# Spectral filter, soft mixture of experts and gated feed-forward on one core: batch sums of the last chain moved to VectorE, weight loads moved to SyncE

## The chip, the cores and the metric

The kernel runs on one core of a Trainium2 chip. The metric is the device time of one execution in microseconds (us), the median over several runs. TensorE does the matrix products, VectorE and ScalarE read its results out of PSUM, GpSimd helps with elementwise work, and SyncE only issues DMA transfers; ScalarE and GpSimd can issue transfers too, each from its own queue, in program order with their other instructions.

## The reference

Cut to what matters (shapes: x 8 x 3072 x 256, w1 8 x 256 x 1024, w2 8 x 1024 x 256, gate and value weights 256 x 1536, output weights 1536 x 256):

```
Y = irfft(rfft(x, axis=1) * (filt_r + 1j * filt_i))      # per batch, along the sequence
x = Y.reshape(8 * 3072, 256)
logits = x @ phi                                          # 32 slots
d = exp(logits - logits.max(0)); d /= d.sum(0) + 1e-9     # over all 24576 tokens
slot_input = (d.T @ x).reshape(8, 4, 256)                 # 8 experts, 4 slots each
slot_out[e] = relu(slot_input[e] @ w1[e]) @ w2[e]
c = exp(logits - logits.max(1)); c /= c.sum(1) + 1e-9
x = c @ slot_out
out = (silu(x @ w_gate) * (x @ w_val)) @ w_out
```

## The kernel before, in words

The program is one list of instructions for each engine, in the order in which the Python code emits them. Nothing is reordered at run time: an engine works through its list and waits where a tile is not ready.

**Phase 1** (`phase1`, to 350 us) is the spectral part. 16 steps (batch and half of the columns) have 6 units each, so `units` has 96 entries `i`. `s2_unit` multiplies and filters, `tr_unit` and `phi_pair` transpose and form logits in the spectral domain two units later, `s1_chunk` prepares the next step. Beside the units a generator `chain(b, last)` runs for each batch: it is cut by `yield` into pieces, and `pump(1)` emits the next piece. The pieces are, in order: six transposes (tile `lh`, L354), a product with `inv` (L364, `us`), six transposes (`t4`), the logits (L391, then the maximum `cm` at L398 and the copies `lg`), the batch maximum `mb` (L411), subtraction and exponential (`dd`), a product back (L447, transposed into `bd`), a product with `fwd` (L459, `dt`), six transposes (L474, `dh`), and the slot product of 48 matrix instructions in six parts `k` with the batch's filtered rows `yt` (L482, copied to `sl`). Batches 0 to 5 store `sl` to DRAM; batch 6 and batch 7 are the two chains g6 and g7 at the end. In the last ten units `pump(1)` is called twice a unit, until g6 has done nine pieces. Behind the loop the two generators are advanced in an order written out by hand, `for g in (g6, g7, g6, g7, g7, g6, g7, g6, g6)`, and then g7 to its end.

The generator `combine()` joins the eight batches: weights exp(mb - max) for each batch, their normalisation, then the scaled sum of the eight `sl`. Before, the sum is made on TensorE: 28 matrix instructions with 32 columns (L548) for batches 0 to 6, and four (L502) that add batch 7. Its result `sp` goes into a block layout `stm`.

The expert weights w1 are 16 halves of 512 KB. 13 of them are issued by ScalarE in units 84, 90 and 91 into buffers that phase 1 has freed there, and 3 by SyncE behind the loop (all at L134). The eight w2 (1024 KB each, L770) are issued by SyncE in the order 6, 7, 0, then the gate weights `wg`, then 5, 4, 1, 2, 3 and the value weights `wv` (1536 KB each, L127). Each waits until the tiles of phase 1 at its address are read for the last time.

**Transition** (`transition`, 378 to 405 us): `stage1` (L812) multiplies the slots by w1, `turn` (L829) transposes, `stage2` (L837) multiplies by w2. Then the slot outputs are multiplied by the gate and value weights (L872, L883) into tiles `g4` and `v4`: rows of a rounded part and of its remainder. For the first 512 columns the remainder is formed on VectorE at L877, for the other 1024 columns 16 transfers (L895) copy the rows into place, 8 issued by SyncE and 8 by GpSimd.

**Phase 2** (`phase2`) has 576 items of 512 tokens x 128 hidden columns. Each: two matrix products G and V (L988, L989), SiLU (L991), product h (L997), split into `hi` and `lo` (L1004, L1005), and six output products (L1026) three or four items later. The output weights come in as 12 tiles; `load_out(f)` rounds one on ScalarE (L977) and forms its remainder on GpSimd (L978), one tile an item in items 0 to 11. The last 12 items end in another layout (`close`): four accumulators, each read by a ScalarE copy (L1060) and a VectorE sum (L1061), then four transfers on SyncE (L1069).

Of the kernel before, what the change touches and what calls it, by code (L numbers as in the profile page):

```python
# [20 lines left out]
NF = FF // 128  # L21
LAG = 4
EXP_AT = 17
HOLD = 9
# [55 lines left out]
def spectral_softmoe_glu_kernel(  # L80
# [56 lines left out]
    def phase1():  # L137
        with ExitStack() as c1:
# [4 lines left out]
            cvp = c1.enter_context(tc.tile_pool(name="cvp", bufs=1))  # L143
# [5 lines left out]
            ps_s1 = c1.enter_context(tc.tile_pool(name="ps_s1", bufs=1, space=PSUM))  # L149
            ps_x = c1.enter_context(tc.tile_pool(name="ps_x", bufs=2, space=PSUM))  # L150
            ps_t = c1.enter_context(tc.tile_pool(name="ps_t", bufs=1, space=PSUM))
            ps_l = c1.enter_context(tc.tile_pool(name="ps_l", bufs=1, space=PSUM))
            ps_c = c1.enter_context(tc.tile_pool(name="ps_c", bufs=1, space=PSUM))
# [154 lines left out]
            def chain(b, last):  # L308
# [15 lines left out]

                def pair(name):
                    if b == NB - 2 and name in ("dt", "dh"):
                        t = ytp.tile([128, 768], F32, tag="yt", name=name)
                        return [t[:, 0:512], t[:, 512:768]]
# [58 lines left out]
                cm = chp.tile([128, E], F32, tag="cm", name="cm")  # L387
# [9 lines left out]
                both = bass.AP(pl[0].tensor, pl[0].offset, [list(pl[0].ap[0]), [16, E], [512, 2], [1, 16]])  # L397
# [10 lines left out]
                if not last:  # L408
                    yield
                ps = small()  # L410
                pe.transpose(out=ps[0:32, 0:128], in_=cm, identity=ident)  # L411
                dve.tensor_reduce(
                    out=mb[:, b:b + 1],
                    in_=ps[0:32, 0:128].rearrange("p (g n) -> p g n", g=2)[:, :, 0:48],
# [22 lines left out]
                if last:  # L437
# [3 lines left out]
                bd = chp.tile([128, E, 32], F32, tag="lg", name="bd")  # L441
                pl = (ps_s1.tile([128, 1024], F32, tag="s1", name="cl") if last else small()).rearrange(
                    "p (g e n) -> p g e n", g=2, n=16
                )
                for h in range(2):
                    for g in range(2):
# [5 lines left out]
                        )  # L452
                for es in es2:
# [3 lines left out]
                for jj in range(NJ):  # L457
# [6 lines left out]
                    )  # L464
                dt_ = evac("dt", ps)
# [7 lines left out]
                for k in range(6):  # L473
                    pe.transpose(out=col(ps, k), in_=col(dt_, k), identity=ident)  # L474
                if last:
                    rb, pss = next(com)
                dh = evac("dh", ps)
                yield
                ps = two(True)[0] if b == NB - 2 else small()
                for k in range(6):  # L480
# [9 lines left out]
                    if k in (2, 5) and b == NB - 2:  # L490
# [5 lines left out]
                act.copy(sl, ps[:, 0:256])  # L496
                if b < NB - 2:
                    nc.scalar.dma_start(out=sld[:, b, :], in_=sl)
                if last:
                    next(com)  # L500
                    for d_ in range(2):
                        pe.matmul(  # L502
                            out=pss[d_][:, 0:32], lhsT=sl[:, d_ * 128:(d_ + 1) * 128], rhs=rb[:, b, :],
                            start=False, stop=True,
                        )
                        (dve.tensor_copy if d_ else act.copy)(sp[:, d_, :], pss[d_][:, 0:32])
# [10 lines left out]
            def combine():  # L517
# [5 lines left out]
                beta4 = chp.tile([128, NB, 1], F32, tag="beta4", name="beta4")  # L523
                dve.tensor_reduce(out=mx, in_=mb, axis=AX.X, op=ALU.max)
                dve.tensor_scalar(al, mb, mx, None, ALU.subtract)
                act.activation(al, al, AF.Exp)
                yield
# [4 lines left out]
                dve.tensor_scalar(al, al, sm, 2.0 / SEQ, ALU.mult, ALU.mult)  # L532
                yield
                rb = chp.tile([128, NB, 32], F32, tag="t4", name="rb")
                psb = ps_t.tile([128, 512], F32, tag="T", name="psb")
                pe.matmul(out=psb[:, 0:NB], lhsT=rep4[0:32, :], rhs=al)
                dve.tensor_copy(beta4[:, :, 0], psb[:, 0:NB])
                dve.tensor_tensor(
                    out=rb,
                    in0=rep4[:, None, 0:32].to_broadcast([128, NB, 32]),  # L540
                    in1=beta4.to_broadcast([128, NB, 32]),
                    op=ALU.mult,
                )
                pss = [ps_x.tile([128, 512], F32, tag="X", name="pss") for _ in range(2)]
                yield rb, pss
                for d_ in range(2):
                    for b in range(NB - 1):
                        pe.matmul(  # L548
                            out=pss[d_][:, 0:32],
                            lhsT=slots[b // 4][:, b % 4, d_ * 128:(d_ + 1) * 128],  # L550
                            rhs=rb[:, b, :],
                            start=(b == 0),
                            stop=False,
                        )
                yield

# [93 lines left out]
            xp += [cr.enter_context(tc.tile_pool(name=f"xp{k}", bufs=1, side="right")) for k in (1, 0)][::-1]  # L650
            load_x(0, 0)
# [52 lines left out]
            for i, (s, u) in enumerate(units):  # L704
# [18 lines left out]
                if (s, u) in ((2 * NB - 2, 0), (2 * NB - 1, 0)):  # L723
                    wt = xp[s % 2].tile([128, 2, 2, FE], F32, tag="x", name="w")
                    for k in range(2):
                        load_w1(nc.scalar, 2 * (s % 2) + k, enumerate(wt[:, k, t] for t in range(2)))
                if (s, u) == (2 * NB - 1, 0):
                    load_w1(nc.scalar, 4, [(t, sgp.tile([128, FE], F32, tag="sg", name="w")) for t in range(2)])
                if (s, u) == (2 * NB - 1, 1):
                    wt = bp[0].tile([128, 3, FE], F32, tag="b", name="w")  # L730
                    load_w1(nc.scalar, 5, ((0, wt[:, 0]), (1, wt[:, 1])))
                    load_w1(nc.scalar, 7, ((0, wt[:, 2]),))
                if i >= len(units) - 10:
# [9 lines left out]
            load_w1(nc.sync, 6, ((0, wt[:, 0]), (1, wt[:, 1])))  # L743
            load_w1(nc.sync, 7, ((1, wt[:, 2]),))
# [4 lines left out]
            for u in (4, 5):  # L749
                tr_unit(2 * NB - 1, u, dve.tensor_copy)  # L750
                next(g7)
            for g in (g6, g7, g6, g7, g7, g6, g7, g6, g6):
                next(g, None)
            for _ in g7:
                pass
# [5 lines left out]
    def transition():  # L761
# [13 lines left out]
        w2s[0] = one([128, 8, D], "w2_0")  # L775

# [9 lines left out]
        one([128, 10 * D], "pad")  # L786
# [8 lines left out]
        for e in (6, 7, 0):  # L795
            load_w2(e)
        flat_load(wg, wd[0], 128)
        for e in (5, 4, 1, 2, 3):
            load_w2(e)
        flat_load(wv, wd[1], 128)  # L800

# [67 lines left out]
        for w, dst in gates:  # L869
# [6 lines left out]
            for r in (32, 96):  # L876
# [262 lines left out]
```

## Time and profile before

| | |
|---|---|
| median of 3 runs | 1464.82 us (1464.5 to 1465.57) |
| the profiled execution | 1466.01 us |
| its span, first to last instruction | 1464.2 us, so 1.81 us lie around it |
| mean granted TensorE clock | 0.992 of full speed |

The span is what the trace explains; all times of the trace are counted from its start. A full clock is 2.4 GHz, and a granted clock of 0.50 is the lower level, 1.2 GHz.

### The profile page before, as it was taken

To read this page: it belongs to the slowest core of one execution; us is meant where nothing else is said; L and a number is where in the kernel's file an instruction comes from. 1 tells how busy PE (TensorE), PEld (TensorE's weight loads), DVE (VectorE), ACT (ScalarE), POOL (GpSimd) and SP (SyncE) were. 2 spreads that over 40 slices of the span, in tenths; PEclk is the share of its full clock that TensorE was granted. 3 is DMA by queue.
4 is the path that set the end of the run, shared out by engine and by line. 5 is a ranking of instruction groups with operands and counts; after the bars stand their busy time and mean duration, and the time that the engine had idled before them with its cause. 6 is when DMAs were issued, how large, how long until landed. Compare 5 with 4: busy or idle time off the path is not lost.

```text
span 1464.2 us, 22633 instructions
## 1 busy us (share of the span) xinstructions
PE 1414.5 (97%) x8446; PEld 1101.4 (75%) x8446; DVE 1147.1 (78%) x1776; ACT 905.0 (62%) x1650; POOL 243.4 (17%) x315
## 2 busy tenths in 40 slices
PE   4899999998999999999999999999999999999998
PEld 2566666665567888888888888888888888888887
DVE  2788888877188878878887897888779878877775
ACT  2466667764266667666766666676666667666664
POOL 0466666663030000000000000000000000000000
PEclk9999999999999999999999999999999999999999
DMA  9979888978721231231131112212210320221111
GB/s 230 158 121 165 148 135 145 185 156 338 281 50 19 37 67 24 37 61 30 30 59 40 29 31 56 40 29 44 55 29 15 73 40 16 54 47 21 24 29 30
DMA packets 178077, 116.26 MB, mean 79 GB/s; under 512 B 105136, under 2 KB 161328, under 8 KB 177840
## 3 DMA queue, kind: packets, MB, share of 16 engines
q1 hardware_dynamic: 170720, 102.37, 35.6%
q10 hardware_dynamic: 6800, 11.54, 2.7%
q8 instruction: 67, 1.10, 0.3%
q0 software_dynamic: 448, 0.92, 0.2%
q14 instruction: 42, 0.34, 0.1%
HBM read 68.13 MB, written 34.60 MB: 70 GB/s over the span
## 4 chain that ended last, share of the span: by engine, by line
PE 91%; DVE 4%; ACT 2%; DMA 1%; issue 1%; POOL 1%; SPq 0%; ACTq 0%; POOLq 0%; DVEq 0%
PE o L1026 52%; PE V L989 9%; PE G L988 9%; PE X L258 5%; PE s L230 4%; PE T L283 2%; PE L L291 1%; PE c L482 1%; DMA x<-in_x_dram 1%; DVE sg L238 1%; PE o L1048 1%; PE c L364 1%; DVE P L262 1%; PE h L812 1%; PE c L447 1%
## 5 line engine op out<-in xcount | busy, mean ns | idle before, releaser
L1026 PE MATMUL o<-hi,wo 128*128 128x512 f32 x2256 | 696.3, 390 | 2.7 <-POOL wo L978 2.7
L991 ACT ACTIVATE s<-G 128x512 f32<-128x512 f32 x576 | 344.7, 598 | 331.7 <-PE G L988 327.6
L997 DVE TENSOR_TENSOR h<-V,s 128x512 f32<-128x512 f32 x576 | 393.5, 683 | 154.6 <-ACT s L991 151.8
L1026 PEld LDWEIGHTS o<-hi,wo 128*128 128x128 f32 x2256 | 424.5, 188 | 91.3 <-POOL wo L978 3.0
L1026 PE MATMUL o<-lo,wo 128*128 128x512 f32 x1128 | 439.5, 390 | 0.0
L1005 DVE TENSOR_TENSOR lo<-h,hi 128x512 fp32r<-128x512 f32 x576 | 421.5, 732 | 1.1
L1004 ACT CAST hi<-h 128x512 fp32r<-128x512 f32 x576 | 354.2, 615 | 36.4 <-DVE h L997 35.1
L1026 PEld LDWEIGHTS o<-lo,wo 128*128 128x128 f32 x1128 | 212.0, 188 | 43.9
L989 PE MATMUL V<-c,v 128*128 128x512 f32 x576 | 224.9, 390 | 1.2 <-DVE h L997 1.2
L988 PE MATMUL G<-c,g 128*128 128x512 f32 x576 | 224.7, 390 | 0.3 <-ACT s L991 0.3
L258 PEld LDWEIGHTS X<-fwd,b 128*128 128x128 f32 x768 | 95.2, 195 | 57.0 <-issue 40.3
L989 PEld LDWEIGHTS V<-c,v 128*128 128x128 f32 x576 | 108.4, 188 | 25.0 <-DVE h L997 2.7
L988 PEld LDWEIGHTS G<-c,g 128*128 128x128 f32 x576 | 108.2, 188 | 24.4 <-ACT s L991 1.1
L238 DVE STREAM_TRANSPOSE sg<-s 128x1024 f32<-128x1024 f32 x64 | 78.9, 1236 | 58.4 <-PE s L230 56.7
L258 PE MATMUL X<-fwd,b 128*128 128x128 f32 x768 | 111.6, 289 | 2.2 <-ACT b L247 1.2
L935 POOL TENSOR_TENSOR lg<-lg,mx 96x1024 f32<-96x1024 f32 x7 | 16.8, 2405 | 550.3 <-DVE mx L933 550.3
L230 PE MATMUL s<-x,csm 48*64 48x512 f32 x512 | 73.7, 632 | 18.6 <-DMA x<-in_x_dram 16.6
L247 ACT COPY b<-sg 128x768 f32<-128x768 f32 x64 | 59.0, 925 | 52.8 <-DVE sg L238 52.6
L271 POOL TENSOR_TENSOR yt<-P 128x256 f32<-128x256 f32 x96 | 70.4, 734 | 117.7 <-DVE P L262 117.2
L1031 DVE STREAM_TRANSPOSE ot<-o 128x512 f32<-128x512 f32 x94 | 65.1, 714 | 29.6 <-PE o L1026 29.6
L262 DVE TENSOR_TENSOR P<-X,ft 128x512 f32<-128x512 f32 x96 | 64.6, 672 | 12.0 <-PE X L258 11.8
L273 POOL TENSOR_TENSOR yt<-Q 128x256 f32<-128x256 f32 x95 | 69.5, 731 | 0.2
(202 smaller groups left out, 969.6 us busy)
## 6 DMA issues: line engine op xcount, KB each, us to landing
out_dram<-ot SPq DMA_DIRECT2D x192, 128.0 KB, 2.8
x<-in_x_dram SPq DMA_DIRECT2D x60, 384.0 KB, 8.2
w<-in_moe_w_dram SPq DMA_DIRECT2D x8, 1024.0 KB, 10.2
w<-in_moe_w_dram ACTq DMA_DIRECT2D x13, 512.0 KB, 6.9
c<-ch SPq DMA_DIRECT2D x42, 128.0 KB, 2.4
c<-cl SPq DMA_DIRECT2D x42, 128.0 KB, 2.4
raw<-in_moe_w_gate_dram SPq DMA_DIRECT2D x12, 256.0 KB, 5.2
raw<-in_moe_w_val_dram SPq DMA_DIRECT2D x12, 256.0 KB, 5.8
```

What stands on the lines that cost most here:

```text
L230: pe.matmul(out=ps[64 * k:64 * k + 64, 16 * r:16 * r + 16, :], lhsT=s1t_sb[64 * r:64 * r + 48, :], rhs=xt[step][64 * r:64 * r + 48, k, :, ...
L238: dve.transpose(out=sg.rearrange("p j d k -> p d j k"), in_=ps.rearrange("p n d -> p d n"))
L258: pe.matmul(out=ps[:, g].rearrange("p r m -> p (r m)"), lhsT=bb[:, j, :], rhs=fwd[:, j, :])
L262: dve.tensor_tensor(out=P, in0=ps, in1=f, op=ALU.mult)
L271: pool.tensor_tensor(out=y[:, :, 0, :], in0=P[:, :, 0, :], in1=P[:, :, 1, :], op=ALU.subtract)
L988: pe.matmul(out=pg, lhsT=g4[c][:, fs], rhs=c4[b][:, q, G, :])
L989: pe.matmul(out=pv, lhsT=v4[c][:, fs], rhs=c4[b][:, q, G, :])
L991: act.activation(s, pg, AF.Silu)
L997: dve.tensor_tensor(out=h, in0=pv, in1=s, op=ALU.mult)
L1004: act.copy(hi, h)
L1005: dve.tensor_tensor(out=lo, in0=h, in1=hi, op=ALU.subtract)
L1026: pe.matmul(out=a[h], lhsT=w[:, k, h], rhs=m, start=(f == 0 and n == 0), stop=(f == NF - 1 and n == 2), skip_group_check=True,)
```

## The change

- **Batch sums on VectorE.** `combine()` no longer multiplies on TensorE. The weights go to all partitions by one small product, and a new function `add(b)` sums batches 0 to 6 in place in the tile of slot outputs, seven VectorE instructions of 128 x 256 placed between the pieces of g7. Batch 7 is added by the instruction that reads its slot product out of PSUM. The normalisation is applied in `rb`, now one block for all batches, and four matrix instructions (L502) form `sp`.
- **The slot product of batch 6** is yielded in six parts, and the order by hand becomes `(g6, g7, g6, g7, g7, g6, g6, g7, g6, g7, g6, g7, g6, g6, g7)`. The second `pump(1)` of a unit stays in units 86 to 88 alone.
- **PSUM and buffers of the last chains.** Two banks of the finished `s1` stage become two separate tiles for g7's pieces; the logit maximum is taken by halves while ScalarE copies the other half; the transposes of the last two units are read by ScalarE.
- **Weight loads.** All w1 halves are issued by SyncE, in units 84, 88, 89, 90 and behind the loop. Expert 6 gets the space of the weight conversion, which moves to the other side of the memory. The w2 order becomes 6, 7, `wg`, 5, 1, 4, 2, 3, `wv`, 0, and expert 0 takes a space that the last chain's rows `yt` use until its slot product.
- **Gate copies.** One 64-row instruction in place of two of 32 rows at L877; 12 of the 16 row copies on SyncE and 4 on GpSimd. `load_out` for tiles 0 to 2 moves ahead of them.
- **End.** The last two items are done together, accumulator by accumulator, each read as soon as it is complete; the output goes out in eight transfers of half the size on SyncE, GpSimd and ScalarE.

```
-                    ps = ps_s1.tile([128, 1024], F32, tag="s1", name="cl")
-                    return [ps[:, 0:512], ps[:, 512:1024]]
+                    return [ends[0].tile([128, 512], F32, tag=f"e{k}", name="cl") for k in range(2)]
...
-                dve.tensor_reduce(out=cm, in_=both, axis=AX.XY, op=ALU.max)
                 for h in range(2):
-                    act.copy(lg[h], pl[h].rearrange("p (e n) -> p e n", n=16))
+                    if last:
+                        dve.tensor_reduce(out=cm[:, h], in_=plv[1 - h], axis=AX.X, op=ALU.max)
+                    act.copy(lg[h], plv[h])
...
-                    if k in (2, 5) and b == NB - 2:
+                    if k < 5 and b == NB - 2:
                         yield
...
-                act.copy(sl, ps[:, 0:256])
+                if last:
+                    rb, beta4, acc = next(com)
+                    dve.scalar_tensor_tensor(sl, ps[:, 0:256], beta4[:, b:b + 1], acc, ALU.mult, ALU.add)
+                else:
+                    act.copy(sl, ps[:, 0:256])
...
+                psb = ps_l.tile([128, 512], F32, tag="L", name="psb")
+                pe.matmul(out=psb[:, 0:NB], lhsT=rep4[0:32, :], rhs=al)
+                yield
+                dve.tensor_copy(beta4, psb[:, 0:NB])
+
+                def add(b):
+                    row = slots[b // 4][:, b % 4, :]
+                    if b == 0:
+                        dve.tensor_scalar(row, row, beta4[:, 0:1], None, ALU.mult)
+                    else:
+                        acc = slots[0][:, 0, :]
+                        dve.scalar_tensor_tensor(acc, row, beta4[:, b:b + 1], acc, ALU.mult, ALU.add)
...
-                yield rb, pss
-                for d_ in range(2):
-                    for b in range(NB - 1):
-                        pe.matmul(
-                            out=pss[d_][:, 0:32],
-                            lhsT=slots[b // 4][:, b % 4, d_ * 128:(d_ + 1) * 128],
-                            rhs=rb[:, b, :],
...
+                psn = ps_l.tile([128, 512], F32, tag="L", name="psn")
+                pe.matmul(out=psn[:, 0:1], lhsT=rep4[0:32, :], rhs=sm)
+                rb = chp.tile([128, 32], F32, tag="t4", name="rb")
+                nrm = chp.tile([128, 1], F32, tag="nrm", name="nrm")
+                dve.tensor_copy(nrm, psn[:, 0:1])
+                dve.tensor_scalar(rb, rep4[:, 0:32], nrm, 2.0 / SEQ, ALU.mult, ALU.mult)
+                for b in range(2, NB - 2):
+                    add(b)
+                yield
+                add(NB - 2)
+                yield rb, beta4, slots[0][:, 0, :]
...
-                if i >= len(units) - 10:
+                if len(units) - 10 <= i < len(units) - 7:
                     pump(1)
...
-            for g in (g6, g7, g6, g7, g7, g6, g7, g6, g6):
+            for g in (g6, g7, g6, g7, g7, g6, g6, g7, g6, g7, g6, g7, g6, g6, g7):
                 next(g, None)
...
-            for r in (32, 96):
-                dve.tensor_tensor(out=dst[r:r + 32, :], in0=pg[r:r + 32], in1=dst[r:r + 32, :], op=ALU.subtract)
+            dve.tensor_tensor(out=dst[64:128, :], in0=pg[64:128], in1=dst[64:128, :], op=ALU.subtract)
+        for f in range(EARLY):
+            later["load_out"](f)
...
-                (nc.sync if r < 2 else nc.gpsimd).dma_start(
+                (nc.sync if r % 2 or c == 2 else nc.gpsimd).dma_start(
...
+        def close(two):
+            ...
+            for t in range(4):
+                for i in two:
+                    part(i, t)
+                a = acc[0][t]
+                tmp = kp.tile([128, D], F32, tag="tmp", name="tmp", bufs=4)
+                act.copy(tmp, a[:, D:2 * D])
+                dve.tensor_tensor(...)
+                if t % 2:
+                    for ii in range(4):
+                        (nc.sync if ii % 2 == 0 else nc.scalar if t == 3 else nc.gpsimd).dma_start(...)
```

## Rows read from the trace of the kernel before

**Rows 1.** The page: busy time and share of each engine.

```profile
PE 1414.5 (97%) x8446; PEld 1101.4 (75%) x8446; DVE 1147.1 (78%) x1776; ACT 905.0 (62%) x1650; POOL 243.4 (17%) x315
```

**Rows 2.** Stretches: length, busy time of each engine, granted clock, DMA share, GB/s.

```profile
362.00:364.00 2.00, 2.00 (x12) 0.58 (x8) 1.00 (x3) 0.21 (x1) 0.44 (x1) 0.50 1.03 418
...
376.00:378.00 2.00, 2.00 (x18) 1.90 (x17) 0.00 (x0) 0.18 (x1) 0.00 (x0) 1.00 1.02 408
...
380.00:382.00 2.00, 2.00 (x12) 0.45 (x8) 0.00 (x0) 0.00 (x0) 0.00 (x0) 0.50 1.02 406
...
414.00:416.00 2.00, 2.00 (x6) 1.60 (x5) 1.07 (x2) 1.41 (x3) 0.74 (x1) 0.50 0.00 0
```

**Rows 3.** Waits of PE from 300 and 379 us: total, times, longest.

```profile
PE c L447 <- DVE Q L263: 1.1, 1, 1.1
...
PE o L1026 <- POOL wo L978: 2.7, 1, 2.7
```

**Rows 4.** The chain that ended last, 350 to 389 us: start, us, what.

```profile
350.81 0.45 PE cl L354 x2
...
364.75 2.72 PE cl L482 x24
367.47 1.90 PE cl L459 x48
...
371.57 2.75 PE c L482 x48
374.32 3.24 PE pss L548 x28
...
378.67 7.03 PE h L812 x48
...
386.37 1.85 PE h L812 x16
...
388.90 1.86 PE o L837 x32
```

**Rows 5.** Timeline of VectorE, 344 to 367 us: start, us, instruction, idle before.

```profile
344.98 0.41 DVE L303 TENSOR_TENSOR lts<-lts,L 128x256 f32<-128x256 f32 x1
...
364.80 1.31 DVE L349 STREAM_TRANSPOSE bd<-cl 128x512 f32<-128x512 f32 x2 [1.76 <-PE cl L447]
```

**Rows 6.** DMA issues from 359, 367 and 371 us: KB, us to landing.

```profile
lgd<-lg POOLq DMA_DIRECT2D x4, 96.0 KB, 5.9
...
w<-in_moe_w_dram SPq DMA_DIRECT2D x5, 1024.0 KB, 9.7
...
wv<-wvd SPq DMA_DIRECT2D x1, 1536.0 KB, 16.6
```

**Rows 7.** Timeline of ScalarE and of SyncE's queue, 310 to 373 us.

```profile
340.72 0.59 ACT L284 COPY y<-T 128x512 f32<-128x512 f32 x1 [2.22 <-PE T L283]
...
367.65 3.66 SPq L770 DMA_DIRECT2D w<-in_moe_w_dram  x5
371.42 0.44 SPq L127 DMA_DIRECT2D wv<-wvd  x1
```

**Rows 8.** Timeline around the first items of phase 2.

```profile
404.82 0.50 PE L988 MATMUL G<-c,g 128*128 128x512 f32 x1
...
407.69 0.69 DVE L1005 TENSOR_TENSOR lo<-h,hi 128x512 fp32r<-128x512 f32 x1
...
410.00 2.78 POOL L978 TENSOR_TENSOR wo<-wo 128x256 fp32r<-128x256 f32 x4
410.30 3.04 DVE L1005 TENSOR_TENSOR lo<-h,hi 128x512 fp32r<-128x512 f32 x1
...
418.43 0.39 PE L988 MATMUL G<-c,g 128*128 128x512 f32 x1
```

**Rows 9.** Timeline of the end, 1457 to 1464 us, and its DMA issues.

```profile
1459.73 1.73 SPq L1069 DMA_DIRECT2D out_dram<-ot  x4
out_dram<-ot SPq DMA_DIRECT2D x8, 128.0 KB, 2.2
```

More of the change, by code (lines that the diff above doesn't have):

```diff
@@ L23 @@
 EXP_AT = 17
+EARLY = 3
 HOLD = 9
@@ L440, in chain @@
                 yield
[L441 to L444, printed above, removed]
+                bd = chp.tile([128, E, 32], F32, tag="t4" if last else "lg", name="bd")
+                pl = small().rearrange("p (g e n) -> p g e n", g=2, n=16)
                 for h in range(2):
@@ L452, in chain @@
                         )
+                if last:
+                    next(com)
                 for es in es2:
@@ L464, in chain @@
                     )
+                if last:
+                    next(com)
                 dt_ = evac("dt", ps)
@@ L474, in chain @@
                     pe.transpose(out=col(ps, k), in_=col(dt_, k), identity=ident)
+                dh = evac("dh", ps)
                 if last:
-                    rb, pss = next(com)
-                dh = evac("dh", ps)
+                    next(com)
                 yield
-                ps = two(True)[0] if b == NB - 2 else small()
+                ps = ps_t.tile([128, 512], F32, tag="T", name="cl") if b == NB - 2 else small()
                 for k in range(6):
@@ L499, in chain @@
                 if last:
-                    next(com)
                     for d_ in range(2):
-                        pe.matmul(
[L503 to L506, printed above, removed]
+                        pss = ps_x.tile([128, 512], F32, tag="X", name="pss")
+                        pe.matmul(out=pss[:, 0:32], lhsT=sl[:, d_ * 128:(d_ + 1) * 128], rhs=rb)
+                        (dve.tensor_copy if d_ else act.copy)(sp[:, d_, :], pss[:, 0:32])
                 for u in range(6):
@@ L650, in phase1 @@
             xp += [cr.enter_context(tc.tile_pool(name=f"xp{k}", bufs=1, side="right")) for k in (1, 0)][::-1]
+            cvp = cvs.enter_context(tc.tile_pool(name="cvp", bufs=1, side="right"))
             load_x(0, 0)
@@ L924, in first, with load_out @@
                 )
+        def load_out(f):
+            st = wo[f][:, 1, :].bitcast(F32)
+            act.copy(wo[f][:, 0, :], st)
+            pool.tensor_tensor(out=wo[f][:, 1, :], in0=st, in1=wo[f][:, 0, :], op=ALU.subtract)
         def build(b):
@@ new lines, in part @@
+        def part(i, t):
+            f = items[i][3]
+            a = acc[0][t]
+            ts = slice(128 * t, 128 * t + 128)
+            pe.matmul(
+                out=a, lhsT=hhi[i][:, ts], rhs=wo[f].rearrange("p k d -> p (k d)"),
+                start=(f == 0), stop=(f == NF - 1), skip_group_check=True,
+            )
+            pe.matmul(
+                out=a[:, D:2 * D], lhsT=hlo[i][:, ts], rhs=wo[f][:, 0, :],
+                start=False, stop=(f == NF - 1), skip_group_check=True,
+            )
@@ new lines, in rows @@
+        def rows(i):
+            accs(i)
+            for t in (2, 3, 0, 1):
+                part(i, t)
+            hhi.pop(i)
+            hlo.pop(i)
+        def close(two):
+            b, q, G, _ = items[two[0]]
+            row = b * SEQ + 1024 * q + 16 * G
+            ot = kp.tile([128, 4, D], F32, tag="ot", name="ot", bufs=2)
+            for t in range(4):
+                for i in two:
+                    part(i, t)
+                a = acc[0][t]
+                tmp = kp.tile([128, D], F32, tag="tmp", name="tmp", bufs=4)
+                act.copy(tmp, a[:, D:2 * D])
+                dve.tensor_tensor(
+                    out=ot[:, t].rearrange("p (m h) -> p h m", h=2),
+                    in0=a[:, 0:D].rearrange("p (h m) -> p h m", h=2),
+                    in1=tmp.rearrange("p (h m) -> p h m", h=2),
+                    op=ALU.add,
+                )
+                if t % 2:
+                    for ii in range(4):
+                        (nc.sync if ii % 2 == 0 else nc.scalar if t == 3 else nc.gpsimd).dma_start(
+                            out=bass.AP(out.tensor, (row + 4 * ii + t - 1) * D, [[32 * D, 32], [1, 2 * D]]),
+                            in_=ot[32 * ii:32 * ii + 32, t - 1:t + 1].rearrange("p t d -> p (t d)"),
+                        )
@@ L1079, in lag @@
             return min(LAG, 3 + i // 10)
-        todo = list(range(len(items)))
+        todo = list(range(len(items) - 2))
         gen = build(1)
```

145 lines of the change are left out of this document (58 added, 87 removed).

## The prediction

> **What bounds the kernel now.** Read the page first: PE is busy 97% of the span [rows 1], so time can only come from stretches in which PE waits, does work that need not be there, or runs at a lower clock. The waits of PE by stretch find few of them: one of 1.1 us in the last units, a handful of tenths around the last chain, and one of 2.7 us at the start of phase 2 [rows 3]; behind 470 us that view lists none, so the long middle will stay as it is. The stretches with the granted clock then show the second loss: from 362, 380 and 414 us PE is "busy" 2.00 us of every 2.00 at clock 0.50, which is 1.2 GHz [rows 2]. The chain that ended last [rows 4] shows the third: 3.24 us of small products (L548) between the last slot product and the expert layers. All that the change touches lies in these places and behind the last matmul.
>
> **Last units.** L447 of batch 6 stands in PE's list before the exponential that feeds it is ready, 1.1 us [rows 3] (the row names the last VectorE instruction, but the operand comes from ScalarE). With one piece a unit from unit 89 on, a whole unit of PE work comes between the two. Bounds 0 to 1.1; I take **1.0**. ScalarE also loses its 13 weight issues; that is worth nothing, since ScalarE waited 2.22 us for PE between them, and not the other way [rows 7]. SyncE takes them, behind the logit store of batch 6 and ahead of the loads of `slots`; those are first read by `add`, some 25 us later, which is their cover.
>
> **Start of the last chain.** The six transposes went to one double bank, so ScalarE's copy waited for the last two, 0.45 us [rows 4]; two tiles free it. **0.45**. The maximum by halves gives nothing more: two reductions of about half a length follow each other as the one did, and the copies that now run beside it are ready no later than the batch maximum.
>
> **The slot product in six parts.** Before, its second half (2.72 us at the low clock) stood ahead of L459, which started at 367.47 [rows 4], while its operand `bd` was done at 364.80 + 1.31 = 366.11 [rows 5]: 1.36 us too late. After, one part fills the wait for `bd`, one the wait between L459 and L474. The last two stand ahead of the last slot product; at 2.75 / 6 = 0.46 us a part [rows 4] they take 0.92, while PE before had 2.2 us from the end of L459 (369.37) to 371.57, of which the transposes filled less than half. Gain between 0 (the low clock lasts until it has eaten the head start) and 1.4; I take **0.6**.
>
> **Sums on VectorE.** L548 goes: 3.24 us [rows 4]. In its place stands one VectorE instruction of 128 x 256 that reads PSUM. The trace has none with this operation; the nearest, an addition of the same size out of PSUM, takes 0.41 [rows 5]. With the hand-overs to and from PE I count 0.7 (bounds 0.5 and 1.0): **2.5**. The seven others cost 7 x 0.41 = 2.9 us of VectorE. They lie beside L459, L474 and the slot products of both batches, a stretch of some 8 us in which VectorE did little before; the last one needs batch 6's `sl` and should end 1 us ahead of the last slot product. If that cover fails, up to 1.3 us of them show.
>
> **First expert layer.** Its first 48 instructions took 7.03 us, at the low clock at first, and the next 16 took 1.85 [rows 4]; 48 at that rate are 5.55. So 1.5 us hang on the clock. It fell behind L548, in which PE was busy 2.00 of 2.00 us, but with matmuls of 32 columns [rows 2]. Those are gone, and the dense slot product comes right ahead. Bounds 0 and 1.5; I take **1.2**.
>
> **The late weights.** So far 5.75 us are won up to the second expert layer, which began at 388.90 [rows 4]. Now w2 of expert 0 comes last on SyncE and waits for the last slot product. Before, five w2 and `wv`, 6656 KB, were issued from 367.65 and the last landed at 371.42 + 16.6 = 388.0 [rows 6, 7]: 20.4 us. After, expert 2's load can go once part 3 has run, near 368, and 4608 KB remain from there: 14.1 us in proportion, 15.3 if some 4 us are fixed, so the last lands at 382.1 to 383.3. It is wanted at 388.90 - 5.75 = 383.15. A near tie; I count **-0.35**. What is left: **5.4**.
>
> **Start of phase 2.** PE waited 2.7 us for the remainder of output tile 0 [rows 3], which GpSimd formed only at 410.00, behind its eight row copies [rows 8]; then the clock was low until about 416. After, tiles 0 to 2 are ready early, in a gap of ScalarE, which had nothing to do before PE ended L883, and the first output product waits for `lo` at 407.69 + 0.69, 3.6 us behind the first G (404.82). G of item 4 follows; V of item 4 needs row copies issued last, worth about +6.1; item 1 needs its `lo`. There GpSimd's four copies end near +3.5 and four subtractions follow in one block: in the row, `lo` took 3.04 us against 0.69 while such a block of 2.78 ran [rows 8]. So `lo` of item 1 comes at +7.0, and with 1.8 an item (576 items between 404.82 and about 1459 [rows 8, 9]) G of item 6 stands at +10.3, against 418.43 - 404.82 = 13.6 before: 3.3 us. If PE's waits again bring the low clock, up to 2.7 of it go (5.4 us of work at half speed, as before). Bounds 0 and 4.0 (no block); I weigh that fall at a third: **2.4**. L877 saves 1.4 us of VectorE, hidden behind L883.
>
> *A rule beside these rows.* What held `lo` is a question of which VectorE instructions suffer. The Trainium skill (SBUF — State Buffer, "Who interferes with whom") says that VectorE contends with a GpSimd instruction that reads SBUF only where VectorE has two SBUF inputs. By it the three early subtractions, beside instructions that read one operand from PSUM, delay nothing. Were every VectorE instruction held, the row copies would start 2.2 us later and the 3.3 would be 1.6; by the rule they stay 3.3.
>
> **End.** Four transfers followed the last sum on SyncE, 1.73 us of issue or 0.43 each [rows 9]. After, the last pair of accumulators goes out by two on SyncE and two on ScalarE, the rest earlier: two issues, **0.85**, bounds 0.4 and 1.3. PE's work is the same, and the last sum ends as late after it as before; a half-sized transfer I count at the same 2.2 us.
>
> **The sum.** 5.4 + 2.4 + 0.85 = 8.65 us. Against the profiled execution: 1464.2 - 8.65 = 1455.55 of span, with 1.81 around it 1457.4. The median of the runs lies 1.2 under the profiled time, so **1456.2 us**. A measurement of this kernel tells about 0.2%, 2.9 us, from no change.
>
> **The rivals.**
> *Clock stays up.* The low clock of 362 us ends sooner, none falls at 404 to 416, and the weights land early: 1.0 + 0.45 + 1.4 + 2.5 + 1.5 + 4.0 + 0.85, so about 11.7, 1453.1. For it: dense products replace small ones. Against: waits of up to 1.3 us were enough near 360, and the pieces there stay small. The Trainium skill (TensorE: Matmul & The Clock Gate, "Why this matters for your kernels") blames idle gaps between bursts, and by it this rival would be the likeliest; the trace disagrees, for at 378 the clock fell behind 2.00 of 2.00 busy us [rows 2]. Chance 0.15.
> *Weights or clock take back.* Expert 0's weights land 1 to 2 us late (1.5), L812 runs low again (the 1.2 counted), phase 2 starts at the low clock (2.4 becomes 3.3 - 2.7 = 0.6): with all three 8.65 - 1.5 - 1.2 - 1.8 = 4.15, 1460.7, with two of them about 1459.4. For it: the tie above. Chance 0.18.
> *Nothing comes of it.* The sums show on VectorE (1.3), the six parts give nothing (0.6), and all of the rival before comes on top: 4.15 - 1.9 = 2.25 left, 1462.6, within what can be told. Chance 0.06.
> *Slower: one queue for all.* SyncE now works through every load in order. Expert 4's w2 waits for GpSimd's logit stores (5.9 us to land [rows 6]), since they read a tile at its address, and behind it queue experts 2 and 3, `wv` and expert 0. To end slower by 2.9, expert 0 would have to land at 388.9 + 3.25 + 2.9 = 395, so expert 2's load would have to be issued after 379.7; the stores were issued from 359 on, so they were done by 368. Price from there on 1 us for each us, 1468 at the point where it can be told. Chance 0.04.
> The forecast itself: 0.57.
>
> **How the numbers follow.** The forecast's own range is 1454.3 to 1458.5. Going out to the rivals on either side, to 1452.7 below (clock up with the full end term) and 1460.9 above (late weights and low clock with the bounds of the sums), leaves out the last two and some edges, under 2 in 10. Faster by more than 0.2%: 0.57 + 0.15 + 0.18 less an edge of 0.01, 0.89; within 0.2%: 0.07; slower: 0.04.
>
> **What would show it.** No wait of PE ahead of L447 before 349 us; L459 of g7 right behind `bd`; no L548, and the first L812 some 1.9 us behind the end of the last slot product; L812's first 48 in 5.6 us; the first L837 near 383.5, ahead of it a wait for expert 0 of at most 0.5; G of item 6 some 10 us behind the first G, with one long `lo`; the last transfer issued 1.35 us, not 2.2, behind PE's end. The forecast fails if the first L837 waits for DMA by more than 2 us, if a `next` order lets L474 or the last slot product wait for parts 3 to 5 at the low clock, or if the granted clock is 0.50 in a stretch where it was 1.00.

## The result, and the profile after

The changed kernel is slower: 1477.34 us in the median against 1464.66 for the kernel before beside it, a ratio of 1.0087 (95% interval 1.0074 to 1.0100). That is 12.7 us more, where 8.6 less was forecast, and 16.4 above the upper end of the range. Its profiled execution took 1476.74 us, with a span of 1474.9. The waits of PE, read first (what waited, for whom; us in total, times, longest):

```profile
PE o L861 <- DMA w<-in_moe_w_dram: 13.2, 1, 13.2
PE G L1013 <- ACT s L1016: 8.5, 2, 8.2
PE L L294 <- DVE lts L306: 1.3, 1, 1.3
PE c L456 <- DVE dd L445: 1.0, 1, 1.0
```

The two waits of [rows 3] are gone, and two larger ones stand at other places. (L456 is the product that was L447; its 1.0 us is that of batch 7, in the last chain.) PE's timeline around them (start, us, instruction; in brackets the idle time before it):

```profile
367.11 1.91 PE L495 MATMUL c<-y,dha 128*32 128x256 f32 x32
370.50 0.63 PE L519 MATMUL pss<-rb,sl 128*128 128x32 f32 x4 [0.61 <-DVE sl L511]
371.74 5.36 PE L836 MATMUL h<-w,stm 128*32 128x512 f32 x48 [0.61 <-DVE stm L828]
...
393.47 3.64 PE L861 MATMUL o<-w,ht 128*32 128x256 f32 x32 [13.16 <-DMA w<-in_moe_w_dram]
...
412.02 0.50 PE L1013 MATMUL G<-c,g 128*128 128x512 f32 x1
...
421.41 0.79 PE L1013 MATMUL G<-c,g 128*128 128x512 f32 x1 [8.19 <-ACT s L1016]
```

Until 380 the change does more than was forecast: the first expert layer (L812 before, L836 now) starts 6.9 us earlier, and its first 48 products take 5.36 in place of 7.03 [rows 4]. Then its second layer (L837, now L861) stands 4.6 us later than before. Lengths of the stages, each from one start in PE's timeline to the next, in us; "mended" is the run e4_pairs below:

| Stage | before | changed | mended |
|---|---|---|---|
| start to the small product of `mb` of batch 6 | 334.53 | 334.19 | 335.99 |
| to the last product with `phi_sb` (last units) | 15.04 | 13.61 | 13.60 |
| to the first layer (last chain) | 29.10 | 23.94 | 23.94 |
| to the second layer | 10.16 | 21.73 | 8.50 |
| to the first G | 15.99 | 18.55 | 15.99 |
| to the G of item 6 (start of phase 2) | 13.61 | 17.89 | 9.36 |
| to the end | 1045.77 | 1044.99 | 1044.92 |
| span | 1464.2 | 1474.9 | 1452.3 |

The first row says nothing of the change: over the 14 profiles it lies between 334.2 and 338.4, and e4_pairs and e8_best_again, one kernel, have 336.0 and 338.4. So a stage is read from its own row, not from the difference of two times.

For the first wait, the queue of SyncE, what it waited for, and the row of the chain that ended last:

```profile
356.18 13.33 SPq L794 DMA_DIRECT2D w<-in_moe_w_dram  x5
369.55 0.50 SPq L128 DMA_DIRECT2D wv<-wvd  x1
370.14 0.44 SPq L794 DMA_DIRECT2D w<-in_moe_w_dram  x1
379.74 0.82 SPq L940 DMA_DIRECT2D c<-cd  x2
```

```profile
SPq L794 <- PE cl L495: 10.7, 1, 10.7
```

```profile
370.14 23.19 DMA w<-in_moe_w_dram
```

Expert 5's load goes at 356.18. Expert 1's then waits 10.7 us, until batch 6's whole slot product has run, and everything behind it goes between 367.4 and 370.2, expert 0 as the last. It takes 23.2 us to land. The stretches show the rest (length, busy time of PE, PEld, DVE, ACT, POOL, granted clock, DMA share, GB/s):

```profile
360.00:364.00 4.00, 3.47 (x62) 1.85 (x62) 2.73 (x8) 0.21 (x2) 0.00 (x0) 1.00 1.01 412
364.00:368.00 4.00, 3.76 (x68) 2.34 (x64) 2.63 (x11) 2.01 (x5) 0.00 (x0) 1.00 0.22 88
...
380.00:384.00 4.00, 0.31 (x3) 0.12 (x1) 1.04 (x2) 0.00 (x0) 0.00 (x0) 1.00 1.02 396
384.00:388.00 4.00, 0.00 (x0) 0.00 (x0) 0.00 (x0) 0.00 (x0) 0.00 (x0) 0.68 1.05 274
388.00:392.00 4.00, 0.00 (x0) 0.00 (x0) 0.00 (x0) 0.00 (x0) 0.00 (x0) 0.50 1.06 248
```

While SyncE stood, the DMA engines ran dry (share 0.22 in 364 to 368). From 384 they are full as well but move 274 and 248 GB/s in all, in place of some 400: the row transfers of `c`, issued at 379.7, run beside the weights. PE is idle from 380.3, and the clock falls to 0.50.

For the second wait, ScalarE's first SiLU and the last row copies of SyncE:

```profile
420.76 0.60 ACT L1016 ACTIVATE s<-G 128x512 f32<-128x512 f32 x1 [8.01 <-DMA v<-gh]
```

```profile
412.77 0.60 SPq L920 DMA_DIRECT2D g<-gh  x1
...
419.43 1.15 SPq L920 DMA_DIRECT2D v<-gl  x2
```

The first G was done at 412.5, and its SiLU waits for a copy out of `gh`, with which it has no data in common. What they share is bytes. Added up from the code, `gh` starts at byte 51200 of a partition before; with w2 of expert 0 (8192 bytes) moved behind it, at 43008. Phase 2's work tiles (`kp`) take bytes 0 to 45056, so all 2048 bytes of `gh` lie under them.

### The profile page after: what moved, and what is told of

It is laid out like the page before. It is cut to its first block, busy times and chain, and to the rows that moved or that the text cites. A ratio compares the mean times of both kernels' runs of the same rounds, so it can differ in the third digit from the quotient of the medians.

```text
span 1474.9 us, 22608 instructions
## 1 busy us (share of the span) xinstructions
PE 1407.5 (95%) x8421; PEld 1096.7 (74%) x8421; DVE 1143.6 (78%) x1781; ACT 906.1 (61%) x1651; POOL 242.2 (16%) x313
## 4 chain that ended last, share of the span: by engine, by line
PE 86%; DVE 5%; DMA 4%; ACT 2%; issue 1%; POOL 1%; SPq 1%; ACTq 0%; DVEq 0%; POOLq 0%
PE o L1051 52%; PE V L1014 9%; PE G L1013 9%; PE X L261 4%; PE s L233 4%; PE T L286 2%; DMA w<-in_moe_w_dram 2%; DVE sg L241 1%; PE L L294 1%; DMA x<-in_x_dram 1%; PE c L495 1%; PE o L1071 1%; DVE P L265 1%; PE o L861 1%; PE c L369 1%
## 5 line engine op out<-in xcount | busy, mean ns | idle before, releaser
L1014 PEld LDWEIGHTS V<-c,v 128*128 128x128 f32 x576 | 108.4, 188 | 24.5 <-DVE h L1022 2.4
```

The costliest lines, as they stand in the source:

```text
L1014: pe.matmul(out=pv, lhsT=v4[c][:, fs], rhs=c4[b][:, q, G, :])
```

## The experiments

The twelve runs, with the waits of PE for expert 0's weights and for the SiLU, in us (an empty cell: not in question there; e8, e10 and e11 are kernels measured a second time):

| Run | median us | ratio to before (95%) | weights | SiLU |
|---|---|---|---|---|
| e1_order | 1466.39 | 1.0001 (0.9989 to 1.0014) | 1.3 | 10.2 |
| e2_home | 1470.36 | 1.0035 (1.0021 to 1.0049) | 13.2 | 0.3 |
| e3_order_home | 1457.53 | 0.9947 (0.9928 to 0.9966) | 1.2 | 1.9 |
| e4_pairs | 1453.56 | 0.9919 (0.9901 to 0.9938) | none | 0.3 |
| e5_pairs_old_order | 1460.25 | 0.9976 (0.9963 to 0.9990) | 0.5 | 0.3 |
| e6_no_early | 1457.29 | 0.9947 (0.9934 to 0.9959) | none | 0.3 |
| e7_sums_on_pe | 1457.43 | 0.9949 (0.9935 to 0.9962) | | |
| e8_best_again | 1454.03 | 0.9931 (0.9913 to 0.9948) | none | 0.3 |
| e9_shift_2kb | 1458.65 | 0.9949 (0.9932 to 0.9965) | 1.1 | 1.7 |
| e10_old_order_again | 1462.15, one run | | 5.7 | |
| e11_before_again | 1466.33, one run | | | |
| e12_c_later | 1471.65 | 1.0044 (1.0028 to 1.0060) | 7.4 | 8.4 |

**e1_order**, against the changed kernel:

```diff
-        for e in (5, 1, 4, 2, 3):
+        for e in (5, 1, 2, 3, 0, 4):
             load_w2(e)
         flat_load(wv, wd[1], 128)
-        load_w2(0)
```

> Only the order of the loads differs from the changed kernel: experts 2, 3 and 0 go ahead of expert 4 and wv. Theory 'last in line': the wait of 13.2 us at the first L861 is there because expert 0's w2 is the last of 6656 KB that SyncE can only issue from 367.4 on. By it expert 0 has 4096 KB to share with; at the 6656 KB in 20.4 us of the kernel before that is 12.6 us, so it lands at 380 to 384, the wait falls to 0 to 4 us, and the time by 8 to 11 us, to 1466 to 1469. Rival 'the home or the other transfers': expert 0's new place in SBUF, or the row transfers of c, make that one load slow (23.2 us); then the wait stays above 8 us and the time above 1472.

**e2_home**, against the changed kernel:

```diff
+        w2s[0] = one([128, 8, D], "w2_0")
         ht = [[one([128, 4, 128], f"ht{i}{k}") for k in range(2)] for i in range(2)]
...
-        w2s[0] = one([128, 8, D], "w2_0")
         one([128, 2 * D], "pad")
```

> Only the place of expert 0's w2 in SBUF differs from the changed kernel: it stands ahead of the transposed activations again, so gh and gl lie outside the bytes that phase 2's work tiles take. Theory 'address': the first SiLU waits 8.0 us for the 16 row copies because its pool takes the bytes of gh and gl. By it the wait of the G of item 2 (8.5 us) falls to under 1 us and the time by 6 to 8.5 us, to 1468.5 to 1471.5. Rival 'copies': twelve copies on SyncE are simply late for what reads them; then PE waits for copied rows in its place, 4 us or more, and the time stays above 1473. On the first L861 the wait of about 13 us stays in both, if the place is not what makes that load slow.

**e3_order_home** has both edits.

> Both edits: the order of the loads, and the place of expert 0's w2. If each wait has the cause named, the gains add: 14 to 19 us below the changed kernel, 1458 to 1463, which is faster than the kernel before by 2 to 7 us. If one cause hides the other (a late start of phase 2 that would be late anyway), it is one gain alone, 1466 to 1471.

The waits of PE in e1_order, then in e2_home:

```profile
PE G L1012 <- ACT s L1015: 10.2, 2, 9.9
...
PE o L860 <- DMA w<-in_moe_w_dram: 1.3, 1, 1.3
```

```profile
PE o L861 <- DMA w<-in_moe_w_dram: 13.2, 1, 13.2
...
PE G L1013 <- ACT s L1016: 0.3, 1, 0.3
```

Each edit takes away its own wait and leaves the other: 11.0 us for the order, 7.0 for the place, 19.8 for both (as differences of the ratios to the kernel before, 0.9, 0.5 and 1.4%). So expert 0's new place did not make its load slow, and twelve copies on SyncE are not late for those who read them. In e1_order the SiLU waits 1.7 us longer than in the changed kernel, and this is a third wait, which neither the forecast nor the theory of the address has: ScalarE rounds the three early output tiles ahead of `gh`, and now that PE comes there earlier, ScalarE stands for their transfer `wo`:

```profile
401.33 1.02 ACT L952 CAST wo<-wo 128x256 fp32r<-128x256 f32 x3 [1.97 <-DMA wo<-wod]
```

So SyncE's first row copy goes 2.3 us behind the first G there, and 0.75 behind it in the changed kernel.

**e9_shift_2kb**, against e1_order, puts the theory of the bytes alone to the test:

```diff
+        one([128, 2 * D], "pad")
         gh = one([128, 512], "gh", dt=F32R)
         gl = one([128, 512], "gl", dt=F32R)
         w2s[0] = one([128, 8, D], "w2_0")
-        one([128, 2 * D], "pad")
```

> The new order of the loads with expert 0's place left where the changed kernel has it, behind gh and gl; but an unused tile of 2048 bytes a partition, which stood behind it, stands ahead of gh. So gh starts at byte 45056, where phase 2's work tiles (45056 bytes) end. Theory 'address': these 2048 bytes are the whole cause; the wait of the third G for the first SiLU falls from 9.9 us to under 2 us, and the time to that of the run with both edits, 1456.5 to 1460. Rival 'place of expert 0': with w2 of expert 0 behind gh and gl something else holds the SiLU back; the wait stays above 7 us and the time above 1464.

The wait falls from 10.2 to 1.7 us with nothing changed but the place of an unused 2048 bytes, and the time is within 1.2 us of e3_order_home. The overlap is the cause of all but the 1.7 us; with these goes ScalarE's wait for `wo`, 1.74 us here and 1.89 in e3_order_home, where the SiLU waits 1.9.

**e12_c_later**, against the changed kernel, asks what the transfers of `c` add:

```diff
-        later["first"]()
...
         turn(1, 0)
+        later["first"]()
...
-                (nc.sync if r < 2 else nc.scalar).dma_start(
+                nc.scalar.dma_start(
...
-                nc.sync.dma_start(
+                nc.scalar.dma_start(
```

> The changed kernel with one edit: the four row transfers of c and the three of wo, which it issues at 379.7 and 380.6 while expert 0's w2 is still under way, are issued from ScalarE behind the copy of the third set of transposed activations, so not before the first L861 has run. Order, place and pools of the loads are those of the changed kernel. Theory 'collision': at 384 about 0.7 MB of the 6.8 MB of weights is left, which alone takes 2 us at 410 GB a second; beside the 1.6 MB of c, which drop the rate to 250 to 275, it takes 9. With c later expert 0 lands at 385 to 387, the wait at the first L861 falls from 13.2 to 5 to 7 us, and the time by 6 to 9 us, to 1468 to 1471. Rival 'place in line alone': the wait stays above 11 us and the time within 2 us of the changed kernel's. The wait for the first SiLU, some 8 us, stays in both; if c or wo then come late for phase 2, a wait of PE for c shows ahead of the first G, up to 4 us.

The wait falls to 7.4 us, a little more than the 5 to 7 expected, and the time by 5.7, a little less than the 6 to 9. The stretch in which the rate had dropped, and the chain's row, now read:

```profile
384.00:388.00 4.00, 0.00 (x0) 0.00 (x0) 0.08 (x1) 0.00 (x0) 0.00 (x0) 1.00 1.01 410
```

```profile
373.12 17.51 DMA w<-in_moe_w_dram
```

So 5.8 of the 13.2 us are the collision with `c` (and with `wo`, moved along with it). The 7.4 left are the stall behind the pool and the place in line, which this run does not separate; the order alone, in e1_order, leaves 1.3 even beside `c`, so the shares overlap. Why the rate drops shows later in the same trace, when no weights are under way and `c` comes with the start of `wo`:

```profile
400.00:404.00 4.00, 2.95 (x34) 1.55 (x27) 0.42 (x1) 1.86 (x3) 0.00 (x0) 1.00 1.04 205
```

The DMA engines are full and move 205 GB/s. From 406 to 408, with `c` landed, `wo` runs at 348. So the row transfers of `c` fill the engines with about half the bytes that the weight loads move in the same time; whether the mixture of the two adds to that is not shown.

**e4_pairs**, against e3_order_home, gives each two y tiles a pool of their own:

```diff
-            yp = [c1.enter_context(tc.tile_pool(name=f"yp{k}", bufs=1)) for k in range(3)]
+            yp = [c1.enter_context(tc.tile_pool(name=f"yp{k}", bufs=1)) for k in range(7)]
...
-                    yt[b, u] = yp[1 + (k >= 8)].tile([128, 4, D], F32, tag=f"y{k}", name="y")
+                    yt[b, u] = yp[k // 2].tile([128, 4, D], F32, tag=f"y{k}", name="y")
```

> As with both edits, and the y tiles stand in seven pools of two instead of three pools, so that a load can start when its own two tiles have been read and need not wait for a whole pool. Theory 'release by pool': SyncE's stall on expert 1's load, 10.7 us until 367.4, becomes short (expert 1 issued near 359, expert 2 near 365), about 2 MB less stand in line at 367.4, expert 0 lands by 381 and the wait at the first L861 is under 0.5 us; 1 to 4 us below the run with both edits, 1455 to 1461. Rival 'by tile already' (the forecast's assumption: the load waits for what it needs alone): the issue times do not move, and the time is that of both edits within 1 us.

SyncE's waits, its issues of expert 5 and 1 and of expert 2, and one stretch:

```profile
SPq L794 <- PE cl L495: 9.8, 3, 5.5
```

```profile
357.97 3.05 SPq L794 DMA_DIRECT2D w<-in_moe_w_dram  x2
...
366.65 0.37 SPq L794 DMA_DIRECT2D w<-in_moe_w_dram  x1
```

```profile
364.00:368.00 4.00, 3.22 (x68) 2.45 (x64) 2.49 (x10) 1.27 (x4) 0.00 (x0) 1.00 1.03 414
```

One wait of 10.7 has become three, of which the longest is 5.5. Expert 1's load goes within 3.1 us of expert 5's, the DMA engines stay full, and no wait for weights is left. So in three pools a load waited for the last reader of a whole pool, not for that of its own tiles. The rival "by tile already" is out: against e3_order_home the time falls by 4.0 us, and the runs of the two do not overlap.

**e5_pairs_old_order** keeps the pools and the place, with the loads in the changed kernel's order; **e10_old_order_again** is the same kernel in another execution.

> The y tiles in pools of two and expert 0's place mended, but the loads in the changed kernel's order: 5, 1, 4, 2, 3, wv, and expert 0 last. This is the case that the forecast counted on (each load goes once its own tiles are read). The forecast's near tie: expert 0 lands within 1.5 us of the time at which the first L861 wants it, and the time is within 1.5 us of the kernel with the new order. Theory 'last in line': even so the transfers run at their full 410 KB a us until 384 in the kernel with the new order, and what comes last then shares with the row transfers of c at some 265; so expert 0, wanted at 382, lands at 384 to 388, PE waits 2 to 6 us, and the time is 2 to 8 us above the kernel with the new order, 1456 to 1462.

> The kernel with pools of two, the place mended and the old order once more. Its profiled execution had the low clock from 363 to 371, so PE came to the first L861 2.1 us late and waited only 0.5; its median was 6.2 us above that with the new order. Theory 'last in line': in an execution without that fall PE comes earlier and waits 2 to 6 us for expert 0. Rival: the wait stays under 1 us whatever the clock did, and the 6 us are elsewhere.

The first profile misses its expectation: 0.5 us of wait, because the low clock in the last chain brought PE there later. The second, without that, shows it:

```profile
388.42 3.53 PE L861 MATMUL o<-w,ht 128*32 128x256 f32 x32 [5.72 <-DMA w<-in_moe_w_dram]
```

With the wait come 1.6 us more for these 32 products (1.93 in e4_pairs). The medians of e5 and e8 lie 6.2 us apart, which is nearer to the 7.4 us that the second profile loses from the first layer to the first G (31.9 against 24.5) than to the 0.6 of the first; how often each occurs no trace shows.

**e6_no_early**, against e4_pairs, undoes the three early output tiles (`EARLY = 0`):

> From the best kernel so far (loads in the new order, place of expert 0, pools of two), the three early output tiles alone are undone: their split is formed in phase 2's loop as in the kernel before. The forecast's step: the first output product waits for GpSimd's remainder again, 2.7 us, and the clock falls once; the G of item 6 comes 12 to 14 us behind the first G in place of 9.4, and the time is 2.4 to 4.3 us above that kernel, 1456 to 1458. Rival 'hidden anyway': with 12 of the 16 row copies on SyncE, GpSimd is free early enough by itself; under 1 us.

The first G starts at 396.54 and that of item 6 at 409.41: 12.9 us behind it, in place of 9.4, and the median is 3.3 us above that of e8_best_again, taken beside it. The ranges of the two ratios overlap, so the 3.5 us of the stage are the firmer number. The wait is split:

```profile
PE o L1050 <- DVE lo L1029: 1.9, 1, 1.9
...
PE o L1050 <- POOL wo L953: 0.7, 1, 0.7
```

**e7_sums_on_pe**, against e4_pairs, puts the 28 small products back:

```diff
-                    rb, beta4, acc = next(com)
-                    dve.scalar_tensor_tensor(sl, ps[:, 0:256], beta4[:, b:b + 1], acc, ALU.mult, ALU.add)
+                act.copy(sl, ps[:, 0:256])
...
+                    for b in range(NB - 1):
+                        pe.matmul(
+                            out=pss[d_][:, 0:32],
+                            lhsT=slots[b // 4][:, b % 4, d_ * 128:(d_ + 1) * 128],
+                            rhs=rb[:, b, :],
+                            start=(b == 0),
+                            stop=False,
+                        )
```

> From the best kernel so far, the batch sums alone go back to TensorE: 28 small products behind the last slot product, and no sums on VectorE. The forecast's steps: 2.5 us for the sums, and up to 1.7 for the clock in the first expert layer, whose 48 products then take 7.0 us in place of 5.4; so 2.5 to 4.2 us above that kernel, 1456 to 1458. Rival 'the clock is not theirs': the clock stays at 1.00 behind the 28 products, the 48 take 5.4, and the loss is 2 to 3 us. Rival 'no gain in the sums': VectorE is as long; under 1 us.

```profile
371.93 3.31 PE L569 MATMUL pss<-rb,slots 128*128 128x32 f32 x28
375.07 0.61 PE L516 MATMUL pss<-rb,sl 128*128 128x32 f32 x4
376.34 7.05 PE L838 MATMUL h<-w,stm 128*32 128x512 f32 x48 [0.66 <-PE pss L516]
```

```profile
372.00:376.00 4.00, 3.69 (x32) 3.57 (x32) 0.19 (x1) 0.56 (x2) 0.00 (x0) 1.00 1.01 393
376.00:380.00 4.00, 3.66 (x20) 1.27 (x24) 0.20 (x1) 0.00 (x0) 0.00 (x0) 0.57 1.04 425
```

From the first part of the slot product (359.84) to the first layer it takes 16.50 us, in e4_pairs 14.01: 2.5 for the sums. The 48 products behind them take 7.05 again, not 5.36, with the clock at 0.57 in 376 to 380: 1.7 more. The median is 3.4 us above that of e8_best_again, with ranges that overlap; the stages are clearer. In all three profiles with the 28 products (the two of the kernel before and this one) the 48 take 7.03 to 7.05 us, in all eleven without them 5.36, whatever the clock did earlier in the chain. The clock is theirs.

**e8_best_again** is e4_pairs once more.

> The kernel with the new order, expert 0's place and pools of two once more, beside the others on the same chip. 0.7 to 1.0 % below the kernel before, 1452 to 1456; no wait of PE at the first L861, and a granted clock of 1.00 from 340 to 440 us.

The time holds, the clock's part does not. The stretch shown above for e4_pairs, here and in the kernel before once more (**e11_before_again**):

```profile
364.00:368.00 4.00, 3.42 (x18) 1.30 (x18) 2.02 (x6) 0.78 (x2) 0.00 (x0) 0.54 1.02 413
```

```profile
364.00:368.00 4.00, 3.99 (x52) 1.41 (x48) 2.20 (x5) 0.38 (x2) 0.33 (x1) 0.81 1.02 419
```

> The kernel before once more, unchanged. If the fall of the clock between 362 and 368 belongs to the kernel before, this execution has it too (granted clock 0.50 beside L447 and L482), and from the last L291 to the first L812 it takes 29.1 us again. If it comes and goes by execution, as in the best kernel (none in one profile, 7 us of it in the other), that stretch takes 27 to 29 us, and part of the 5.2 us that the changed kernel's profile gains there is luck.

The last chain, 29.10 us in the table above, takes 27.24 in this execution of the kernel before; 23.94 in e4_pairs and 26.62 in e8_best_again, which are one kernel. Of the eleven profiles without the 28 products, six have 23.9 and five 25.9 to 26.6. Part of what the changed kernel gains there comes and goes by execution.

## Why the prediction was wrong

**Late weights (counted at -0.35 us): the first step that failed.** It cost 13.2 us of wait and 2.6 of low clock behind it (first L861 to first G: 18.55 against 15.99). Three things in its working did not hold. First, expert 2's load "can go once part 3 has run": the queue stood at expert 1's load, for a whole pool, so that 6656 KB were left at 367.4, as many as before [rows 7]. Second, the load's time was taken in proportion to bytes from a stretch in which nothing else ran beside these loads. In the kernel before, `c` was issued when the weights had landed; now that the first layer ends earlier, it meets them, which is 5.8 us. The forecast had counted the earlier layer as gain alone and not asked what its end sets off. The Trainium skill (DMA: Bandwidth & Descriptors, "Issuing engines are not separate DMA queues") says that transfers of all issuing engines run on the same 16 engines and interleave; the traces agree, for expert 0's load, issued 9.6 us ahead of `c`, takes 23.2 us beside it and 17.5 without (e12, with the same order and pools). Third, there was no tie even on the forecast's own premise: with release by pairs and the old order the wait is 5.7 us and 1.6 of clock (e10), because the DMA engines had a backlog that the proportion left out (their share in e10 is 1.0 from 340 to 392, without a gap) and `c` came in at 382. In e10 expert 2's load does go at 367.4, as forecast, and expert 0 lands 20.8 us later, where 14.1 to 15.3 were counted; the 4 us taken as fixed there stand in no row. The proportion came from a stretch that began with idle engines (their share was 0.35 from 366 to 368 in the kernel before).

The rival "one queue for all", at a chance of 0.04, was right that the one queue would stand at a load and make expert 0 late, but it named another load, expert 4's behind GpSimd's logit stores. In the changed kernel expert 1's load stood for longer and hid that wait; with seven pools it shows (e10):

```profile
SPq L794 <- DMA lgd<-lg: 5.2, 2, 4.6
```

Its price was wrong too: it wanted expert 2's load issued after 379.7 for a landing at 395. The landing came at 393.3 with every load issued by 370.6. The sign by which the forecast was to fail, the second layer waiting for DMA by more than 2 us, is the one that appeared.

**Start of phase 2 (+2.4 us): the second.** Its mechanism was right and is worth more. In e4_pairs the G of item 6 stands 9.4 us behind the first G against 13.6, a gain of 4.25, just over the upper bound; e6 gives 3.3 to 3.5 of it back by undoing the early tiles alone. The forecast looked at instructions and queues and not at addresses: the line that moves `w2_0` was read as a later load, not as 8192 bytes less ahead of `gh`. That cost 8.2 us, and the low clock again (0.50 in 420 to 424), so that 13.61 became 17.89. Nor did it count that the early tiles put ScalarE behind `wo`, which cost 1.7 to 2.0 us of ScalarE's time in e1, e3 and e9 and nothing in e4.

**Where it held.** Last units: 1.0 forecast, 1.4 measured (the wait of 1.10 is gone, and the product behind it took 1.09 in place of 1.60). Sums on VectorE: 2.5 and 2.5. First expert layer: 1.2, and 1.7, shown to hang on L548 by e7. End: 0.85, and 0.8. Split tiles and slot product in six parts (0.45 and 0.6) are not shown; no run undoes them, and they can't be told from the clock: the last chain, 29.10 and 27.24 before, gained 5.2 us between the two first profiles, and between executions that both had some low clock 2.5 (29.10 to 26.62) or 0.6 (27.24 to 26.62). Where the forecast argued from waits of up to 1.3 us near 360, the waits of PE there were 0.54, 0.34 and 0.63; the one of 1.34 stands at 349.6, and the clock was 1.00 for 10 us behind it. The sum without both waits is what e4_pairs shows, 0.8% (0.6 to 1.0%; once more, in e8, 0.7%) below the kernel before and 1.6% below the changed one; that is near the 1453.1 us of the rival "clock stays up", in which nothing was lost at the start of phase 2 and the weights came early. It is no proof of that rival, for e4_pairs has another order, place and pools, and its clock in the last chain was the luck of the execution.

**The rules beside the rows.** In e4_pairs `gl`, with one operand from PSUM, took 0.69 us beside GpSimd's early subtractions, as it had before without them; `lo`, with two from SBUF, took 1.13 there and 3.70 in e6 beside such subtractions, and 0.68 in e6 while GpSimd was idle:

```profile
400.88 1.13 DVE L1029 TENSOR_TENSOR lo<-h,hi 128x512 fp32r<-128x512 f32 x1
...
399.40 3.70 DVE L1029 TENSOR_TENSOR lo<-h,hi 128x512 fp32r<-128x512 f32 x1
```

Not every such pair shows it on VectorE: in e4_pairs the next two `lo` took 0.67 in the middle of GpSimd's block, in which six subtractions took 6.39 us, 1.07 each, where four in e6 took 2.77. So the rule on VectorE and GpSimd (the Trainium skill, SBUF — State Buffer, "Who interferes with whom") agrees with the traces as far as which instructions suffer, for these operations on two tensors; which of the two engines pays, the forecast did not ask. (The page names copies in a faster mode as well; no row here bears on that.) The rule on idle gaps (the Trainium skill, TensorE: Matmul & The Clock Gate, "Why this matters for your kernels") agrees at both new waits, where PE was idle and the clock went to 0.50; e7 shows again a fall behind busy small products that it does not cover.

## What to carry to other kernels

Loads on one in-order queue go in the order in which they are wanted, and each stands, in this program, behind the last reader of the whole pool whose bytes it takes: write down that reader for every load before moving one. When a stage gets shorter, look up what is issued at its end and what that now meets. When an allocation moves, add up the bytes again, for the tiles that moved with it and for the pool that will lie over them.

## What the runs showed of the hardware

In the changed kernel the DMA engines, full in both cases (share 1.0), moved 396 to 424 GB/s with weight loads alone and 248 to 274 in all once the row transfers of `c` had come beside them; in e12 `c` with the start of `wo` filled them at 205. A stretch of 28 products of 32 columns, PE busy 3.69 of 4.00 us, was followed by a granted clock of 0.57 (e7). A scalar-times-tensor addition of 128 x 256 on VectorE took 0.48 us (L553 and, out of PSUM, L511), where the forecast had taken 0.41 from a plain addition [rows 5]. And one kernel had the granted clock at 1.00 through the last chain in one execution and at 0.54 for 4 us and more in another, with the same instructions; what decides it stays open.
